# Loads of the DFT matrix issued by GpSimd behind the operation that frees their buffer, and a new order list, in a gated mix of a spectral layer and attention

## The chip, the core and the metric

The kernel runs on one core of a Trainium2 chip. Its time is device microseconds of one execution; 1714.48 us is the median of three before the change (1708.18 to 1717.01). The profile comes from one more execution of the same program, which took 1709.57 us, with a span of 1707.8 us from its first to its last instruction. Five engines run side by side, each through its own list of instructions in order: PE (TensorE, the matmuls, with its weight loads shown apart as PEld), DVE (VectorE), ACT (ScalarE), POOL (GpSimd) and SP (SyncE, which here issues DMAs). They wait for one another through semaphores.

## The reference

The output is a mix, by a gate for each row, of two results from the same x of 2048 rows and 640 columns. One is the real part of a two-dimensional DFT, written as matmuls. The other is attention with 32 heads of 20 that share one key and one value.

```python
g = sigmoid((x * gate_w).sum(-1, keepdims=True))
a = x @ dft_hid_re.T
b = x @ dft_hid_im.T
y = dft_seq_re @ a - dft_seq_im @ b
q = (x @ wq).reshape(B, S, 32, 20).transpose(0, 2, 1, 3)
k, v = x @ wk, x @ wv
p = softmax(einsum("bhqd,bkd->bhqk", q, k) * 20 ** -0.5)
o = einsum("bhqk,bkd->bhqd", p, v)
out = g * y + (1 - g) * (o.transpose(0, 2, 1, 3).reshape(B, S, 640) @ wo)
```

All is in float32. The kernel writes a float32 operand as the sum of two rounded parts, high and low, and leaves out the product of the low parts.

## The kernel before

**Stages.** First come the projections q, k, v and the gate, then the DFT over the hidden dimension (line 137), with the first score tiles between them. From 237 to 1537 us runs the main loop, which does three kinds of PE work together. A tail finishes the last head pair and the last DFT groups, and the projection by `wo` ends the program.

**Attention in the main loop.** Heads go in 16 pairs. For each pair the scores are computed twice. The "a" scores (line 363, tokens a to g and A to G of the list) only yield row maxima, by a reduction on DVE (line 370). When a pair's last maximum is there, `a_reduce` and `a_final` put the maxima in order on DVE (lines 389 to 407, result `ms`), `m_d<-ms` writes them to DRAM, and four small loads `qs<-m_d` bring them back as two more rows of the pair's q. The "b" scores (line 877, tokens h to n and H to N) use these rows, so the first b score of a pair waits for its `qs<-m_d`. ACT takes their exponential into `pt` (line 887), and the AV matmuls (line 901, token V) multiply it with v.

**The sequence DFT in the main loop.** The product with the DFT matrix is done in 7 products of half size (`PRODUCTS`), each in 8 groups; the main loop does the first 48 groups (`GMAIN`), the tail the rest. A group uses two halves (`sh` 0 and 1) of a row of blocks of the matrix. For each half, in products 0 to 4, two blocks of 512 KB are loaded into `craw0` and `craw1`, of which there is one buffer each. POOL adds the second to the first (line 522), which frees `craw1`, then makes the high part `ch` (line 532) and the low part `cl` (line 533), which frees `craw0`. Products 5 and 6 have one block a half, in the two buffers in turn. `ch` and `cl` have three buffers each. Below, "a split" is the addition, `ch` and `cl`. Once a group POOL also prepares a tile of x for the next product (lines 560 to 564, "the x part"), and it sums the parts that ACT takes out of PSUM (`ypart`, line 931) and the results in DRAM (`ya`, line 793), which go back by `y_d<-ya`. The DFT matmuls (line 737) take half of PE's rows: token 0 stands for rows 0 to 63, token 1 for rows 64 to 127, and a score on the other half of the rows runs beside them.

**What sets the order.** PE's order in the main loop is written out by hand in `PLAN`, a string of 10,456 characters with one token for each piece of work; "-" ends a part, behind which ACT empties the shared PSUM bank (`epoch`). ACT's, DVE's and POOL's operations stand in the order in which the recording of that list reaches them. DMAs are issued by `move` (line 118), from SP unless told otherwise, and SP issues them one after the other: an issue that waits for a buffer holds up all behind it. `load_c` issues a half's `craw` loads and is called by `f_stream` at the start of each half (line 823) and at its seventh step (line 826); `split_c` is called at its fifth step (line 828).

Of the kernel before, what the change touches and what calls it, by code (L numbers as in the profile page):

```python
# [34 lines left out]
def kernel(  # L35
# [488 lines left out]
    def split_c(g, sh):  # L524
        if g < len(GROUPS):
            eng = nc.vector if g > GMAIN else nc.gpsimd
            add_c(g, sh)
# [5 lines left out]
            eng.tensor_tensor(l, raw, h.bitcast(F32), op=ALU.subtract)  # L533
# [461 lines left out]
    def finish_last(ts, sm):  # L995
# [20 lines left out]
        "VVVVVNfe1i111c11k1h1111n1f11b1l1k1c111h1111fg1E1bVVVVVVV-GMajEdVVVVVVVhC11l1f111nk1bj111a1l111f11g11"
        "b1k111hCVVVV0H00B0N0D00C00M0H0I00G0L00D000000FJA00IgVVVVV-iFAJdeVVVVVVVDhJ0000F000EI0N00DA00C0F0I00l"
        "VVVVVLa11ci1k111m1g1111aI111lc11dnf11111a111blJVVVV-fLJkAnVVVVfJ111lka111g1i1FcVVVVViG0F0KH000jL0B0G"
        "000K00F00A00BcVVVVVVV-AfIklGVVVVIa00MK0E0000NC0H0B0000M0eD00cGVVVVVVVVJd11lm1g11i111a1dj11111e1g1mVV"
        "VV-FjEdiAVVVVVVV1dl1b111hf1111j11ke1g1111b1a1j1f11k111lVVVVV00L0A0I0D00M0000G0LH00C00B00DM0000L00NH0"  # L1020
        "0C00F0I000EVVVV-aJMIG000ED0A00J00000MNB00000ECVVVVVVVVVV1j1e1ig111a1m111j1l111i1d1n111f1h1c111eDVVVV"
        "VV-lHJNfiVVVVVVja11111Gm1l1d11i11jh11111fgVVVVVfJH0NB0000000KEJ00M0A00VVVVV-cDFlGiVVVVVV00I0FD0L0000"
        "N0J00H00FI00E0000DNVVVVVV1n11d1b11l11hm1g11111djl111i111a11111fg1jd11e11VVVV-nCFikHVVVVVVkMB1ja1gEVV"
        "VVVVjAN0M0B0000E000KAJ00000G0I0FVVVV-aJNbdLVVVVB0N00E00K0J0A000I0000G0FK000L0C000A0B0NVVVVVV1h11n11c"
        "i1e111m1a111d1n111c1il111f11hg11VVVVVV-FajLgIVVVVVV11l11gi1h11c11f11l1dg11i111c11h11e11mVVVVVV0C0M0L"
        "000G0A00K0JF000B0LG000000K0H000CFVVVV-GhkBjEVVVV0KG000J000B0L0A00D00GJ000MBeVVVVVVVVB1nf1d1lJ11hVV1e"
        "1m111c1ka11n111em111i1dc111n1111h1f111e1iVV-AcGkFbVVVVVVVVVVVmGC00H00I0K00E00NM00A000J00BVVVVV-iMgAC"
        "kVVVVVVKa00M0J0GB0000L00AK00M0000NJVVVVVVMa11n1d1j111l1ia111mg1111d1cVVVV-mGDBehVVVVVVVd11i111a1l111"
        "n1fk11i11c11la11g11f1111kjVVVVdN00L000FJ0A000I00GK0000L0M0CVVVVV-eDMbgHVVVVVVV00DIH000E00G00MJ00B000"
        "K00000E0MN0A00J0B000K0000EFVVVVVek11111i1fch111111ldn11111f1iac1111l1k1VVVV-HDejBmVVV11cl111m11kb1h1"  # L1030
        "111ge1111jfVVVVVVVVF00J0E000HN0D00000FJ000BH0E0000G0DJ00M0VVVVV-FenJIaVVVVGmJ0L0H000I00D0FnVVVVVVV1i"
        "n1111fa11k111ei1111jg1f1VVVVV-GjLiAdVVVVVhE1b11nd1j11f1111eh111n111icVVVVV0B00LN0J00MA000000B0ED00N0"
        "VVVVVV-eNIfkCVVVVVF00K000CI0G000L000MK00A0I00J00EN00000FAVVVVVf11h1g111j11ie111fh11d1111cn11ie11a111"
        "mVVVVVV-lFCidNVVVVVV1g1kc11i1m1111e11n1d111a1bj11f11l11g11kVVVVVVF00K000BNE00000HM0KC0000G0000BHE000"
        "00MCVVVV-fiAGLkVVVV0LF0H0000K0G00B000LF0A00J0KnVVVVVV1h11gk11mc1111ia111g11k1e1cMVVVVVV-EmgKa11jb111"
        "e1m111k1n11j111a1fVVVVVVVVmA000JG0EK00000BH0M0J00N00D0VVVVVKc00G0I0M00H00E0J000KB000G0FVVV-cIKaNeVVV"
        "VVVVVVVhG1d11j1l1b1111mga1111c1k1l1VVVVVV-AldNcmBVVVVVVc111m11di1na1111j11me111b1d11g11a1111jlVVVVVJ"
        "d00GL0I0000H0F00Ck00000LI0G00FH00000J0D00EG0000IF00HVVVVV-GaBLjdVVVVVVjA0ILG0000D00M0C000H00B000NEVV"
        "VVVVbN111cl1h11f11kn11b111lj11a1111f1d11ig11VVVV-bFkChLVVVVVVFh1lb111jd11n1111am111eb111jVVVVMa0JE00"
        "000IG0K0AmVVVVVV-FhKNbeVVVVVVG00LB00KH000000F00GL000C0DB0000AM0000LNVVVVV1lb1n111d1h11m11e1111b1nc1h"  # L1040
        "d1111m1l11g1b11VVVVV-enDFch11i11l11gVVVVVVVVVGjL0F00IH000K000C0G000E0M00BVVVVVVV-lMBdgHVVVVV0D0H00FN"
        "00I00E00K0AJ00000NM0000IE000K0AVVVVV1ai11f11k111l11g1a1i1c1111k11mg1l1b111a1k111c11fVVVVVV-AiDeCnVVV"
        "VV1n11k11a111eim1gj1111111dh11iVVVVVVI00AK00J0000G000M0IA0D000EN0000J0MH000BVVVVV-MceNAdVVVVVVL00G00"
        "HJ000F0D00000EI000ANcFVVVVVVVh1e1111j11g11i11mae11111j11k1b1g111mh1j111e1k111bf1VVV-jLhGBkVVVVVVVVVk"
        "A00IEN00J00F00H00K000IE000GVVVL00D0n0H0C0B00MVVVV-HcbMnDVVVVVVVdNI0F0J000H000EdGVVVVV1a1k11ec11111n1"
# [212 lines left out]
```

## Time and profile before

| what | us |
|---|---|
| median of three runs | 1714.48 |
| profiled execution | 1709.57 |
| its span | 1707.8 |
| PE, DVE, ACT, POOL busy in the span | 1687.7, 1449.2, 1227.8, 873.1 |
| main loop | 237 to 1537 |
| POOL busy in the main loop | 779.1 |

A row of a timeline gives start, duration, engine, line, operation, output and inputs, and how often; in brackets stands the idle time of the engine just ahead of it and what ended it as far as the profile can tell. A wait that names an engine which had long been done was another, often a DMA. A row of waits gives the total, the count and the longest. Windows give busy time by engine (with the number of instructions), then the granted clock of PE as a share of full speed, the share of time in which the DMA engines were busy, and GB/s. PE's matmuls are pipelined and their ends are modelled.

### The profile page before, as it was taken

How to read it: one execution, taken by the hardware profiler on the slowest of the kernel's cores; microseconds unless marked ns; L12 is line 12 of the kernel's file. 1: busy time of each engine (PE TensorE's matmuls, PEld its weight loads, DVE VectorE, ACT ScalarE, POOL GpSimd, SP SyncE). 2: the span in 40 equal slices, each digit the busy share in tenths (PEclk: the TensorE clock that was granted, in tenths of full speed). 3: DMA queues.
4: the chain of work that ended last, by engine and by line, in shares of the span. 5: the costliest groups of instructions: out<-in, count | busy, mean ns of one | idle time of the engine just before them, and what ended most of it. 6: DMA issues, size and time to landing. Idle time of an engine off the chain costs nothing.

```text
span 1707.8 us, 64072 instructions
## 1 busy us (share of the span) xinstructions
PE 1687.7 (99%) x27862; PEld 1480.6 (87%) x27862; DVE 1449.2 (85%) x2403; ACT 1227.8 (72%) x2499; POOL 873.1 (51%) x599
## 2 busy tenths in 40 slices
...
GB/s 295 239 179 113 149 111 106 109 132 96 133 122 154 125 149 111 152 117 175 110 152 145 161 98 126 134 150 128 161 123 144 94 135 77 106 104 165 207 204 259
DMA packets 139015, 245.38 MB, mean 144 GB/s; under 512 B 26716, under 2 KB 87996, under 8 KB 136212
## 3 DMA queue, kind: packets, MB, share of 16 engines
...
## 4 chain that ended last, share of the span: by engine, by line
PE 92%; DMA 3%; DVE 3%; issue 1%; POOL 0%; SPq 0%; ACT 0%; DVEq 0%; POOLq 0%
PE shared L901 27%; PE shared L737 17%; PE b L877 16%; PE a L363 16%; PE ab L137 7%; PE y_F L737 2%; PE q L126 1%; PE q L128 1%; PE q L127 1%; DVE mx L370 1%; PE av L959 1%; PE o L128 1%; PE o L126 1%; PE o L127 1%; DMA craw<-in_cre_dram 0%
## 5 line engine op out<-in xcount | busy, mean ns | idle before, releaser
L370 DVE TENSOR_REDUCE mx<-a 128x1 f32<-128x512 f32 x2048 | 1260.1, 681 | 112.7 <-PE a L363 85.0
L887 ACT ACTIVATE pt<-b 128x512 f32<-128x512 f32 x2048 | 1051.0, 615 | 215.5 <-PE b L877 153.6
L363 PE MATMUL a<-ks,qs 60*128 60x512 f32 x2048 | 673.3, 397 | 1.5 <-DVE mx L370 0.8
L877 PE MATMUL b<-qs,ks 62*128 62x512 f32 x2048 | 649.6, 397 | 8.3 <-DMA qs<-m_d 7.0
L737 PE MATMUL shared<-x,ch 64*128 64x320 f32 x3072 | 657.0, 301 | 0.3 <-ACT ypart L929 0.3
L737 PEld LDWEIGHTS shared<-x,ch 64*128 64x128 f32 x3072 | 497.7, 186 | 14.5 <-issue 9.1
L901 PE MATMUL shared<-pt,vsb 128*32 128x128 f32 x15360 | 492.7, 275 | 0.1
L901 PEld LDWEIGHTS shared<-pt,vsb 128*32 128x32 f32 x15360 | 399.2, 110 | 84.9 <-issue 49.4
L737 PE MATMUL shared<-x,cl 64*128 64x320 f32 x1536 | 459.6, 299 | 0.0
L877 PEld LDWEIGHTS b<-qs,ks 62*128 62x128 f32 x2048 | 343.7, 185 | 48.4 <-issue 22.4
L363 PEld LDWEIGHTS a<-ks,qs 60*128 60x128 f32 x2048 | 351.8, 185 | 32.3 <-DVE mx L370 11.1
L522 POOL TENSOR_TENSOR craw<-craw 128x1024 f32<-128x1024 f32 x80 | 189.7, 2371 | 242.0 <-DMA craw<-in_cre_dram 120.6
L737 PEld LDWEIGHTS shared<-x,cl 64*128 64x128 f32 x1536 | 285.8, 186 | 4.0 <-issue 2.8
L533 POOL TENSOR_TENSOR cl<-craw,ch 128x1024 fp32r<-128x1024 f32 x98 | 232.5, 2372 | 7.9
L931 POOL TENSOR_TENSOR ypart<-ypart 128x320 f32<-128x320 f32 x72 | 62.7, 871 | 225.8 <-ACT ypart L929 224.4
L532 POOL CAST ch<-craw 128x1024 fp32r<-128x1024 f32 x98 | 101.8, 1039 | 51.1 <-PE shared L737 27.4
L137 PE MATMUL ab<-wh,xh 64*128 64x320 f32 x640 | 124.3, 298 | 1.4 <-DVE both L608 0.9
L137 PE MATMUL ab<-wl,xh 64*128 64x320 f32 x640 | 123.5, 296 | 0.0
L137 PE MATMUL ab<-wh,xl 64*128 64x320 f32 x640 | 123.2, 296 | 0.0
L607 ACT ACTIVATE half<-ab 128x320 f32<-128x320 f32 x64 | 28.0, 437 | 105.6 <-PE ab L137 103.8
L137 PEld LDWEIGHTS ab<-wl,xh 64*128 64x128 f32 x640 | 89.2, 186 | 0.0
L137 PEld LDWEIGHTS ab<-wh,xl 64*128 64x128 f32 x640 | 89.2, 185 | 0.0
...
## 6 DMA issues: line engine op xcount, KB each, us to landing
...
xr<-x_d SPq DMA_DIRECT2D x88, 320.0 KB
...
```

Of the source, the lines that this page charges most:

```text
L126: nc.tensor.matmul(ps, wh, woven(xh), start=(i == 0), stop=False)
L137: nc.tensor.matmul(ps, w[r], woven(x[r]), start=(i == 0 and k == 0), stop=(i == n - 1 and k == 2))
L363: nc.tensor.matmul(ps, qs[p][b : b + 60, qb * P : (qb + 1) * P], woven(ks[b : b + 60, c * ROW : (c + 1) * ROW]), start=True, stop=True,)
L370: return nc.vector.tensor_reduce(mx[p][:, hh, qb, c : c + 1], ps, axis=AX.X, op=ALU.max)
L522: eng.tensor_tensor(raws[0], raws[0], raws.pop(1), op=PRODUCTS[GROUPS[g][0]][0][1])
L532: eng.tensor_copy(h, raw)
L533: eng.tensor_tensor(l, raw, h.bitcast(F32), op=ALU.subtract)
L737: mm = nc.tensor.matmul(ps[g % len(ps)], w, woven(x), start=start, stop=stop)
L877: nc.tensor.matmul(ps, ks[b : b + 62, kc * P : (kc + 1) * P], woven(qs[p][b : b + 62, qc * ROW : (qc + 1) * ROW]), start=True, stop=True,)
L887: halves.scored(nc.scalar.activation(t, ps, AF.Exp, scale=SCALE), n)
L901: mm = nc.tensor.matmul(acc[32 * g : 32 * g + 32], vsb[:, kc], t[:, g * VW : (g + 1) * VW], start=fresh, stop=end)
L931: nc.gpsimd.tensor_tensor(info["t"][0], info["t"][0], t, op=ALU.add)
```

## The change

`load_c` gets an argument for the issuing queue. For groups up to `GMAIN`, `split_c` now issues the next half's loads itself, from POOL: the load into `craw1` right behind the addition that frees it, the load into `craw0` right behind `cl`; where a half has one block, its load goes ahead of or behind the split, depending on the buffer. `f_stream` no longer issues them in the main loop, and still does in the tail. The very first split keeps its loads on SP. And `PLAN` is another string, of the same length and with the same number of each kind of token.

```diff
-    def load_c(g, sh, which=(0, 1), hold=None):
+    def load_c(g, sh, which=(0, 1), hold=None, queue=nc.sync):
...
-                ins = move(raw, (cre, cim)[i][th * SJ + k, sh])
+                ins = move(raw, (cre, cim)[i][th * SJ + k, sh], queue)
...
-    def split_c(g, sh):
+    def split_c(g, sh, ahead=True):
         if g < len(GROUPS):
             eng = nc.vector if g > GMAIN else nc.gpsimd
+            ahead = ahead and g <= GMAIN
+            one = len(c_raw[g, sh]) == 1
             add_c(g, sh)
+            if ahead and not (one and (g + sh) % 2):
+                load_c(g + sh, 1 - sh, which=(1,), queue=nc.gpsimd)
             raw = c_raw.pop((g, sh))[0]
...
             eng.tensor_tensor(l, raw, h.bitcast(F32), op=ALU.subtract)
+            if ahead:
+                load_c(g + sh, 1 - sh, queue=nc.gpsimd)
...
-            split_c(0, 0)
+            split_c(0, 0, ahead=False)
...
-                load_c(g + 1, sh)
+                if g >= GMAIN:
+                    load_c(g + 1, sh)
                 for j in range(SJ):
-                    if j == 6:
+                    if j == 6 and g + sh >= GMAIN:
                         load_c(g + 1 + sh, 1 - sh, which=(1,))
...
-        "hB11jdl111f11n11b111hc11dl1VVVVVCl1h1d11i11gm11lCVVVVmn1BEjkAVVVgI00jL0F000D00H0I0N000C00ME000HD000I"
...
```

Three places show what moves. The first is SP's list around the maxima of pair 8, in the main loop near 920 us of the profile (`craw` are loads of the DFT matrix, `xr` loads of x, `y_d<-ya` stores of results, `m_d<-ms` the store of the maxima). Before:

```order
L118 DMA craw<-in_cre_dram 128x1024 x2
L118 DMA xr<-x_d_70 128x640
L118 DMA xr<-x_d_69 128x640
L118 DMA y_d<-ya 128x320
L118 DMA m_d<-ms 128x64
L118 DMA craw<-in_cre_dram 128x1024
L118 DMA ya<-y_d 128x320
L118 DMA qs_865<-m_d 1x64x32 x4
```

SP's list at the same place now:

```order
L118 DMA xr<-x_d_70 128x640
L118 DMA xr<-x_d_69 128x640
L118 DMA y_d<-ya 128x320
L118 DMA m_d<-ms 128x64
L118 DMA ya<-y_d 128x320
L118 DMA qs_865<-m_d 1x64x32 x4
```

The `craw` loads are gone from SP's list, two ahead of the maxima and one between their store and their loads; the store `y_d<-ya` still stands ahead of `m_d<-ms`.

The second place is POOL's list just ahead of the `ya` that this store takes. Before, two splits follow each other, then the x part and the sums:

```order
L522 TENSOR_TENSOR craw<-craw 128x1024
L532 CAST ch<-craw 128x1024
L533 TENSOR_TENSOR cl<-craw,ch 128x1024
L522 TENSOR_TENSOR craw<-craw 128x1024
L532 CAST ch<-craw 128x1024
L533 TENSOR_TENSOR cl<-craw,ch 128x1024
L560 TENSOR_TENSOR xr<-xr 128x640
L563 CAST x_4_18372<-xr 128x640
L564 TENSOR_TENSOR x_4_18372<-xr,x_4_18372 128x640
L931 TENSOR_TENSOR ypart<-ypart 128x320
L793 TENSOR_TENSOR ya<-ypart,ya 128x320
```

POOL's list at the same place now, from the first of the two splits to the x part:

```order
L522 TENSOR_TENSOR craw<-craw 128x1024
L118 DMA craw<-in_cre_dram 128x1024
L536 CAST ch<-craw 128x1024
L537 TENSOR_TENSOR cl<-craw,ch 128x1024
L118 DMA craw<-in_cre_dram 128x1024
L522 TENSOR_TENSOR craw<-craw 128x1024
L118 DMA craw<-in_cre_dram 128x1024
L536 CAST ch<-craw 128x1024
L537 TENSOR_TENSOR cl<-craw,ch 128x1024
L118 DMA craw<-in_cre_dram 128x1024
L566 TENSOR_TENSOR xr<-xr 128x640
```

Each split issues two loads, and each load stands right behind the operation that frees its buffer; the sums `ypart` and `ya` follow behind the x part as before.

The third place is PE's list up to the first b score of pair 8, `b_8_0_0_1` (the numbers are pair, key block, query block and head of the pair; `a_592_1` is an a score, `x4_3` a tile of x). Before:

```order
L737 MATMUL shared_3908<-x3_3_15521,cl_18112 128x320
L363 MATMUL a_591_1_18849<-ks_82,qs0_863 128x512
L737 MATMUL shared_3908<-x4_3_16033,ch_18367 128x320 x2
L737 MATMUL shared_3908<-x4_3_16033,cl_18368 128x320
L737 MATMUL shared_3908<-x4_3_16033,ch_18367 128x320
L877 MATMUL b_7_14_3_1_18858<-qs1_864,ks_82 128x512
L877 MATMUL b_7_15_3_1_18862<-qs1_864,ks_82 128x512
L737 MATMUL shared_3908<-x4_3_16033,ch_18367 128x320
L877 MATMUL b_8_0_0_1_18867<-qs2_865,ks_82 128x512
```

PE's list up to the same score now:

```order
L743 MATMUL shared_3912<-x3_3_15542,cl_18118 128x320
L363 MATMUL a_588_1_18850<-ks_82,qs0_863 128x512
L743 MATMUL shared_3912<-x4_3_16033,ch_18369 128x320
L884 MATMUL b_7_15_3_1_18854<-qs1_864,ks_82 128x512
L743 MATMUL shared_3912<-x4_3_16033,ch_18369 128x320
L743 MATMUL shared_3912<-x4_3_16033,cl_18370 128x320
L884 MATMUL b_8_0_0_1_18860<-qs2_865,ks_82 128x512
```

In the fourth tile of x the score now comes behind three DFT matmuls instead of five, and behind three fewer a scores of this head (588 instead of 591 is the last ahead of it).

More of the change, by code (lines that the diff above doesn't have):

```diff
@@ L1016 @@
[L1016 to L1045, printed above, removed]
@@ L1111 @@
[L1111 to L1115 removed]
+        "Ai111jdl1m111g111ai1c1111k1l1n11fVVVc11kf1lBGh1VVVVVBh1EmknCVVVVV0D00C0Nl0fI00A00D0N00000C0LF000I00G"
@@ new lines @@
+        "00000H0D0L00I00J000MA00N000E0I0000D0C0H0fVVV-kBhGcLVVVVVVVeNj11a11bk111m1EnVVVbK1m11a1n1ej11111bd11f"
+        "1111hgVVVVVV-dHFbjLVVVVVmC11ek1bh1111g11j111md1111eaVVVVVVVd0L0MG0A00000C0I0D0E0NmVVVV-NcfBkHVVVVVVh"
+        "FK00B0000C0N0LF000000H0IDN0000JL0FaVVVFn1j1k1e11a11b1FgVVVVVVV-IadEmJVVVV1m1d11ja11e1i1111md111j11g1"
+        "1h111ie1f11jDVVVVVjE000FIG000K0A0J0E000B00F0K0VVVVVVV-eKbHCg00M000000K0E00IA000FJ00000KN000B0E0JVVVV"
+        "VVVVVMabj111g11l1k111f11a111ji1e11111n11d11fc11iAVVVVVVV-FkIeCgVVVVVVVlB11j1fd111n1a111l11i1111cn1f1"
@@ new lines @@
+        "1111lkaBVVVVVdMA00L0I000C0G00K000F0L0A00000BJ0D0000NLVVVV-GhbCeMVVVVVViF0JG000H000ED0I00M0C0G000A0Li"
+        "VVVVVIe111ncd11h1m1l1111111gj111h1b11fk111e1gVVVVV-KfLhbJGVVVVVaIe11j1g11111fkAiVVVVViG0M0D000LA0C00"
+        "nB000M000K00EAgVVVVVV-eiKFhCVVVVVKe00FH00IJg00D000E00000HM00BGcVVVVVVVbM11nea111j11d1f1i1111g1l1j1VV"
+        "VV-lDfCiAVVVVVVV1cmb1111h111d11lc1m111g1ia11111e1d111mjVVVVVJ00E0H000FK0G000J00L000A000ID000MJG00000"
+        "L0H0B00D00FVVVV-HbKECM0N0000HB0000D000LF00C00GVVVVVVVVVVgJm11dl1h11111b111n1jf11k1e111i1h1111f1gVVVV"
@@ new lines @@
+        "VV-AgImkLVVVVVV1m11d1n111ei1a1m111k11n11ceBVVVVJG0000E00KI000A000JN00FVVVVVV-nChIeKVVVVVVVV0B00K0LAJ"
+        "000G00B0K00M00A0000LCVVVVVlA1m1c11i11k1g11a1e1111m1j1b11111n1k1a1f1111j1l1gVVV-ChemDIVVVVVVVB11lkfJa"
+        "GVVVM0000D0LJ0A0000B0MG00D000LVVVVVV-NebMdHVVVV0F0I000A0K00N0E0F0I0000C0K000ANL00000BFVVVVVV1blh1111"
+        "fg1111j1111ie1d1fh11111cg1VVVVVV-FkaLjIVVVVVf11j111ail111d11111f1j1ni1111a1k1e1j1111m1gVVVVV0G0MC00K"
+        "0L0000B0G00M0H0D00000CE0I000M0GVVVVVV-EmCbKhVVVM00C00K0H0B0E0000F00C0K00NhBVVVVVGmc1hk1111b11l1gFVVV"
@@ new lines @@
+        "VVVn1e1i1111f11k1jg111111lb111hk1f111g11cVV-FhdBgLVVVVVVVVkE00BM0N00H0000JLD00M0000BG0VVVVVVVV-mNEbj"
+        "KVVVVViGJE000000K0M0A0NB00000J0L0DVVVVJb11d1n1lm111a1111bc111g1ke1VVVVVVV-CkGiFhVVVVg1i1111am11dj111"
+        "g11i1111efh11c111k11b1nVVVVVNfC0K0L00000IA0N00F00D00J0L0VVVVVVV-FeJgbHVVVVVVV0GH000EB0000J0M0000N00A"
+        "0E00CK000M000B00AN000K0E00MVVVVV1f1h111ek111bn11m1111aj1k11e111gi1m11a1VVVV-bnDLAfVVVVV11ld1h11n111b"
+        "111mj11l11d1aVVVVVVAL000C00K00FN0000HE00B0000KJ0G000M0H0E0VVVVV-MglhCBVVNF000eK000JH00BVVVVVViAl1c11"
@@ new lines @@
+        "111dm1n1a111i11e1c1m1VVVVVVVV-CeMBhnVVVm11he11111j1i1g1m11d1111ehVVVVVVVVVaL0M0KB0000GJ0000HE00F0I00"
+        "0DVVVV-HembCNVVVV0F0I000GJL0000A0M000B00D0J00NE0A00F000IVVVVVVVa11i11f1l11n11d11hi111c11l11fg1k111a1"
+        "1cVVVVV-KgAlfBVVVVVV1h1f111l1n1b1111ka1m111e11c1n1i11d111hfVVVV0A0KB000M0J00G00H0K000E000M0B0CN00A00"
+        "0EVVVVVV-AGjFbkVVVVVK00G0MC000H0I000K0000LM0G0CaVVVVVJe11m1n1a1d1i11l1j111m1a111gVVVVVV-fNjAlbd1111n"
+        "11111fja1111lb111nVVVVVVVV0I00AN00000EM00CI00H0G000KmEVVVVVKg0LF000HJ0000B0G0D0E000M0H0VVV-fNHcKbVVV"
@@ new lines @@
+        "VVVVVVVCkhf1111b11n111lc1d1h1111m1gVVVVVV-kFgHcEVVVVVV1n1c11hf11l11d11n1c111a1i1l111f11111knbJVVVVVV"
+        "bNC0M0K000000A0E0N00I0M0C000000KG0A0i00EM00J000D00N0BVVVV-gKclMAbVVVVVFj000HE0KB00000NC000FA000E0KVV"
+        "VVVVVf11h1dj111l11g111m11h1b1c11d1l1n11f11b1VVVV-gkLJmAVVVVVVlGh111cm11kb11111ge11a1j111mVVVVcNL00F0"
+        "00A00KB0jGVVVVVV-IjaKfEVVVVVV0D00M0EJ0000A00I0D0M000NCE0000I0A0F000KVVVVVVa11k11e1m1i1c111111hdn11f1"
+        "11lb1111j11hd1n11111feVVVV1g1-mDhcBlVVVVVVVViE0C0H000K0FN0000E0I000A0J0KVVVVVVVV-KaJBenVVVVV0B0N0E00"
@@ new lines @@
+        "J000K0A00IN00F0000J0L0D00A0I00FVVVVVVVVm11b11l111aj1k111f11i1e11g111ja11k1f111iVVV-DnBAclVVVVVi1111l"
+        "h11g1k1c111b11f11l1111gh11c1d1iLVVVVVVVCL0000DI0000G0M00J000EA000BK0M0000NJ00VVVV-gFHdcLVVVVVVVfLD00"
+        "0N0H00C0B00F000EN00D00HVVVVVV1m1a111lb11k1g1111m1alj1111b111kmg111l1111a111jb11dVVV-AlCmBnVVVVVVVVVI"
+        "g0C00M000HEK00nBVVVLa0D0J0N00I0000MA0L0C000D0G0VVVV-LckfIHVVVVV00MB0dC0H0000LGVVVV1l11c11dh1n111b1e1"
+        "1j1111maVVVVVVV-AFljB1nk111h1111ef1j11111n111i1k1e11af111jVVVVVVVVVJfK00HB00000LN00F0C000D0B00HVVVVV"
@@ new lines @@
+        "VV-dHBcgLVVVVVV0I00CL000DN00H00B0J00E000MD0N000A0I000C000L000MK00GVVVVVGm11j1d11l11ia11gm11111cd1e11"
+        "111h1b1n1m1VVVVV-EgmDhCVVVVVVHgk1fl1111c11b11a1n1k111f11lVVVVVhE0D00IM00000NJ0E0A00B00K00FVVVVV-ikcH"
+        "NEVVVVVVVlA00N0DJ00BF0000H00L0G0000KCVVVVVV1gk1111c1l11f1h11n1d1b11lc111hVVV-eDhIGmVVVViD11h1lgf1111"
+        "j1di111111agVVVVVVVVHbGK0000J00FL00000BH0D0G00J0VVVV-JaKBemVVVVV0I00F0000LDJ0H00B000FG0000EK000C0I00"
+        "0HVVVV11e1h11b1j111nd1m11h1111ecVVVVVVV-dAEiMgVVVVVV1hf1111l11bn111k1a111m1e11c1n1i1k11111a1f1e11g1c"
@@ new lines @@
+        "11iVVVVVLB000M0N00D00C00L000A0IF00N00000KL0C0B0VVVVV-cEkmNAVVVVVVVaN0FLK0000000CB00HN000EF000KVVVVVk"
+        "11e1m111g11i11h1ke11f11c1IgVVVV-IFkejHVVVVVVVV1he1j1111f1k1i1h111e11c11ndFVVVVVGj0K00H0EF000B00J0G00"
+        "0KVVV-JmdIhEVVVVVVV0B0H0LF00000K0J00IA0N00L00F000DVVVVnFd1i1l111c111am11g11i11d1l1VVVVV-gLbdh11fc11n"
+        "11l111111hb1d111111nm1e1111hcVVVVVVVVVCl0AM0000K0N00B0JE000F0000AK0000BGVVVVVVV-AfbKcLVVVVVLF000I000"
+        "0KAJ00EN0000B0M0000K00A0JL00000NB00FVVVVVVg1m1e11i11c1k11111n1f11a1i11e1k11jg11m1VVVVV-jLgmDAVVVVVVm"
@@ new lines @@
+        "d111h11e111n111jm1k11ai11gEVVVVVViGE0000K0MAC000gIVVVV-bHFljKVVVVEI000C000MK0000AL0B000G0M0000CD00A0"
+        "00LIVVVVVVKbl1111ch1g1111mid11111ej11hVVVVVV-JgkhB1lf1111cg1111k1b11a1111meVVVVVVVVVVhB000EM00NDJ000"
+        "0B0H000M000EGVVVVVV-EfgHIcVVVVV0I0F00N00H00EJ0B0K00G0000F000LA0JB0000KVVVVAj11d1m11bl11n11111cafKVVV"
+        "VVVV-AdCnmBVVVVVV11mc11dn111b11h1m1111j1eg1111kh11b11m1111l1c1dg111h1111ifVVVVVVGI00000FKA00L0000N0B"
+        "00J00D0F00LA00000NIVVVV-nFLdaIVVVVVV0B00H00D0LN0000M0I0A000C0LVVVVVjBe1m111a1n111k111bjf111e1n1VVVVV"
@@ new lines @@
+        "-MNcbEkVVVVV1n11d11ie1j11m111nd11i1h11eJVVVVVVHb0E0G0J00KF000000IAVVVVV-FINdejVVVVV00G0K00LC00B000M0"
+        "H000D0GC000LF000IVVVVVVV1j1fb111n111e1kc111m11a1n1VVVV-jGflKBVVVVe11m11d1i111cn11e11m1111hbd1111nj11"
+        "11meVVVVVV00E0MCK000000N0BH000F00E00J000K0G0B0H000F0CVVVVVV-BafNkLVVVVVA00K0L000FN00000IA000KC000LM0"
+        "00G0AVVVVVVa1m1111e1n1dj11111h1mb11n1e11jd11111hi1VVVVV-cNhEfdIVVVVVVi1f11h1k1111e1g1b111m1ac11LkVVV"
+        "VV0L0A000KbF0C0N0L0000A0KVVVVV-JDefaNVVVVV0L0G0000K0M0J000B0L00H0G00D00MVVVVVhDm11e11gj11111ik11a11f"
```

123 lines of the change are left out of this document (49 added, 74 removed).

## The prediction

> **What bounds the kernel now.** I read the page's first two lines, then PE's waits in the main loop, then the clock around its one long wait, then the chain through that wait.
>
> ```profile
> span 1707.8 us, 64072 instructions
> PE 1687.7 (99%) x27862; PEld 1480.6 (87%) x27862; DVE 1449.2 (85%) x2403; ACT 1227.8 (72%) x2499; POOL 873.1 (51%) x599
> PE b L877 <- DMA qs<-m_d: 7.0, 1, 7.0
> PE b L877 <- DVE mx L370: 1.1, 3, 0.5
> PE a L363 <- DVE mx L370: 0.8, 3, 0.3
> ```
>
> PE is busy for 99% of the span, so what a change of queues can win lies in the rest. The last three lines (time, count, longest) are PE's waits between 237 and 1537 us, the stretch that runs by the list PLAN. One is large: 7.0 us, once, for the small loads `qs<-m_d` that bring pair 8's row maxima. All the others come to about 2 us.
>
> ```profile
> 237.00:919.00 682.00, 680.81 (x12509) 592.72 (x12511) 628.33 (x1061) 550.87 (x1139) 413.36 (x269) 1.00 0.44 131
> 929.35:935.20 5.85, 5.85 (x71) 4.92 (x73) 0.69 (x1) 1.36 (x3) 0.00 (x0) 0.50 0.23 43
> 936.00:1537.00 601.00, 599.31 (x11111) 521.38 (x11108) 537.27 (x905) 487.03 (x1005) 357.12 (x249) 1.00 0.43 125
> 237.00:1537.00 1300.00, 1290.15 (x23750) 1122.78 (x23749) 1171.46 (x1975) 1044.01 (x2154) 779.10 (x523) 1.00 0.43 128
> ```
>
> These stretches list busy time of PE, PEld, DVE, ACT and POOL, then the granted clock, the DMA share and GB/s. The clock is 1.00 on both sides and 0.50 for the 5.85 us behind the wait. So the wait costs twice: while PE stands, and again while it runs at half speed.
>
> ```profile
> 921.98 2.36 POOL craw L522
> 924.36 0.33 SPq L118
> 925.22 0.61 SPq L118
> 927.13 2.08 DMA qs<-m_d
> 929.35 0.64 PE b L877
> ```
>
> The chain of waits (start, length, what) goes from an addition on POOL to an issue on SP, further issues, a landing and PE. SP issues in program order, and the issue at 924.36 is a load of the DFT matrix that waited for its buffer. Here is SP's own list, with the rows farther up in which such a load came late:
>
> ```profile
> 841.29 0.48 SPq L118 DMA_DIRECT2D craw<-in_cre_dram  x1
> 854.94 0.42 SPq L118 DMA_DIRECT2D craw<-in_cre_dram  x1
> 874.21 0.43 SPq L118 DMA_DIRECT2D craw<-in_cre_dram  x1
> ...
> 922.05 0.32 SPq L118 DMA_DIRECT2D y_d<-ya  x1
> 922.47 0.38 SPq L118 DMA_DIRECT2D m_d<-ms  x1
> 924.36 0.33 SPq L118 DMA_DIRECT2D craw<-in_cre_dram  x1
> ```
>
> And POOL's list (last bracket: idle time ahead, and who ended it by the profile):
>
> ```profile
> 821.66 0.87 POOL L931 TENSOR_TENSOR ypart<-ypart 128x320 f32<-128x320 f32 x1 [7.02 <-ACT ypart L929]
> ...
> 845.18 2.37 POOL L522 TENSOR_TENSOR craw<-craw 128x1024 f32<-128x1024 f32 x1 [10.23 <-PE b L877]
> ...
> 859.76 2.37 POOL L522 TENSOR_TENSOR craw<-craw 128x1024 f32<-128x1024 f32 x1 [8.65 <-DMA craw<-in_cre_dram]
> ...
> 865.64 1.55 POOL L560 TENSOR_TENSOR xr<-xr 128x640 f32<-128x640 f32 x1
> ...
> 869.56 0.88 POOL L931 TENSOR_TENSOR ypart<-ypart 128x320 f32<-128x320 f32 x1
> 870.52 1.70 POOL L793 TENSOR_TENSOR ya<-ypart,ya 128x320 f32<-128x320 f32 x2
> 878.06 2.38 POOL L522 TENSOR_TENSOR craw<-craw 128x1024 f32<-128x1024 f32 x1 [5.84 <-DMA craw<-in_cre_dram]
> ...
> 910.42 2.36 POOL L522 TENSOR_TENSOR craw<-craw 128x1024 f32<-128x1024 f32 x1 [4.23 <-DMA craw<-in_cre_dram]
> ...
> 921.16 0.86 POOL L793 TENSOR_TENSOR ya<-ypart,ya 128x320 f32<-128x320 f32 x1
> ```
>
> Each of SP's first three rows is followed by the addition that needs it: 841.29 to 845.18 is 3.89 us, 874.21 to 878.06 is 3.85. (The 10.23 us put down to PE are such a load too: line 522 waits for two loads and for nothing of PE.) So POOL lost 10.23, 8.65 and 5.84 us to late loads, fell behind, and reached `ya` at 921.16. SP holds the store `y_d<-ya` ahead of `m_d<-ms`; the maxima had been ready since 909.25:
>
> ```profile
> 909.03 0.22 DVE L407 TENSOR_REDUCE ms<-mt 128x32 fp32r<-128x64 f32 x1
> ```
>
> **The change part by part.** *Loads off SP.* Of 192 `craw` loads 175 move to POOL. SP loses 175 issues and, what counts, their waits in the main loop:
>
> ```profile
> SPq L118 <- POOL craw L522: 260.8, 62, 15.7
> SPq L118 <- POOL cl L533: 213.1, 66, 18.1
> ```
>
> Those 474 us were waits in which everything behind stood. They are no gain in themselves, since PE met only one of them.
>
> *Loads onto POOL.* What an issue costs there is seen in the ten `wraw` loads (group row: count, busy, mean ns; issue rows: KB, us to landing):
>
> ```profile
> L118 POOL DMA_DIRECT2D wraw<-in_wiT_dram x5 | 2.7, 538 | 16.2 <-DVE wl L168 13.7 <-DVE gz L261 2.5
> wraw<-in_wrT_dram POOLq DMA_DIRECT2D x5, 320.0 KB, 8.2
> wraw<-in_wiT_dram POOLq DMA_DIRECT2D x5, 320.0 KB, 4.4
> ```
>
> 175 issues at 0.54 us put 94 us on POOL. It is busy for 779 of 1300 us in the loop, so 867 if all fell there: room is left, and the price to PE is nothing as long as the 521 idle us cover it where they fall. The landing of a 512 KB load issued by POOL isn't in the trace. Below stand SP's 3.85 us for the same load, above it the 8.2 us of the slower `wraw` row. I take 5.5, an estimate: 4.4 for 320 KB, and about 1.1 for 192 KB more, somewhat under SP's 3.85 x 192 / 512 = 1.4, which has a fixed part in it. That keeps to the faster row, since four of the slower row's five were issued within 2.31 us at the start, as no loads of the loop are:
>
> ```profile
> 4.04 2.31 POOL L118 DMA_DIRECT2D wraw<-in_wrT_dram  x4
> ```
>
> *Is POOL in time for pair 8?* I walk its new order from 821.66, where it waited for ACT and so was on time. From the rows: a split with its addition takes 5.9 us (859.76 to 865.64), 7.0 with two issues; the x part 3.9 (865.64 to 869.56); `ypart` and two `ya` 2.7, with one `ya` 1.8. The next addition can start 5.0 us behind a split's end (5.5 less the issue itself). ACT's parts are ready by these rows, and PE's pace is taken as it was:
>
> ```profile
> 854.68 0.43 ACT L929 ACTIVATE ypart<-shared 128x320 f32<-128x320 f32 x1
> ...
> 873.95 0.43 ACT L929 ACTIVATE ypart<-shared 128x320 f32<-128x320 f32 x1
> ...
> 884.11 0.43 ACT L929 ACTIVATE ypart<-shared 128x320 f32<-128x320 f32 x1
> ...
> 907.73 0.54 ACT L929 ACTIVATE ypart<-shared 128x320 f32<-128x320 f32 x1
> ```
>
> Split 822.5 to 829.5, x to 833.4, `ypart` and `ya` to 836.1. Split to 843.1. Split 848.1 to 855.1 (before: from 859.76), x to 859.0, `ypart` and `ya` to 861.7. Split to 868.7 (before: from 878.06); now POOL waits for ACT, until 874.4. `ypart` to 875.3, split to 882.3, x to 886.2, `ypart` and `ya` to 888.9, split to 895.9. Split 900.9 to 907.9 (before: from 910.42), x to 911.8, `ypart` and `ya` to 913.6. Before, `ya` ended at 922.02: the chain to PE starts 8.4 us earlier, and it also loses the load at 924.36, which I count at nothing. PE asked for the maxima at 929.35 - 6.96 = 922.39. The new list has two DFT matmuls and an a score fewer ahead of that score, about 0.5 us of PE's work, so 921.9 is wanted and 929.35 - 8.4 = 920.95 is had. The wait goes, with 0.9 us to spare; landings of over 6.4 us would bring it back.
>
> *The new list.* PE's work is the same: both lists hold 8416 score and DFT tokens and 1920 AV tokens, in 347 AV runs; summing the longer of PE's two row halves in each stretch between runs gives 1,740,992 columns before and 1,740,864 now, 0.01%. Waits fall elsewhere, though. Without that DMA wait PE's waits were about 2 us, so I bound the reshuffle by none (-2) and three times as much (+4), and take 0. DVE, ACT and the tail behind 1537 us keep their operations: 0.
>
> **The sum.** The profiled execution took 1709.6 us, 1.8 more than its span. Minus 7.0 for the wait, minus half of 5.85, or 2.9, for the half clock: **1699.7**. That run lies 4.9 us under the median of three (1714.48), and I add nothing: those runs had the same queue, and a wait a few us longer in them goes too. If the 4.9 have another cause, it is 1704.6.
>
> **The rivals.** *The wait stays.* `y_d<-ya` still stands ahead of `m_d<-ms` on SP. If POOL isn't earlier, because its loads land in 8 us, the same walk ends at 922, and only the issue between `m_d` and `qs<-m_d` goes: 924.36 to 925.22 at most, so 1708.7. For it: the spare is 0.9 us. Against: the rows of 3.85 and 4.4. The Trainium skill (DMA: Bandwidth & Descriptors, section "Issuing engines are not separate DMA queues") speaks for it: all issuers share the same 16 DMA engines, and issuing from several saves only the short time of the issue. By that rule this is the outcome; the 474 us above speak against it, being in-order waits and not issue time. The Trainium skill (DMA: Bandwidth & Descriptors, section "Anatomy of one DMA — SWDGE (gpsimd) path") also fits 2.0 us plus bytes over 436 GB/s for loads from GpSimd, 3.2 us here by estimate, which would raise the spare to 3.2; no run here shows it yet.
>
> *POOL becomes the bound: slower.* In products 0 to 4 POOL has two splits, an x part and the additions for each group, and PE gives it 1300 / 48 = 27.1 us. The splits' 14.0, and twice the wait for a landing (less the 0.5 of the issue), exceed that from a landing of 7.1 us on. At 8.2 it is 29.4, 2.3 more in each of 40 groups, 92 us; three buffers of split data let POOL fall behind by some 20 us first: 1699.7 + 72 = 1772. Against it: the 8.2 us belong to the program's start alone.
>
> *The new list waits elsewhere.* The first score of a pair comes about as soon behind its maxima as before, so any pair can stand where 8 did, for a few us: 1704.
>
> **How the numbers follow.** Forecast 0.68; the wait stays 0.14 (1708.7); waits elsewhere 0.11 (1704); POOL as the bound 0.07. The range runs from 1695 (the -2, and a few waits too short to be listed) to 1709, which takes in two rivals and leaves out the slow one. About 0.5% is what a measurement of this kernel can tell from no change. Against the median, faster means under 1705.9; so faster has the forecast and half of the third case, 0.73, no change the rest of both rivals, 0.19, slower 0.08.
>
> **What would show it.** Right: no DMA wait of PE in the loop, clock 1.00 throughout, `m_d<-ms` issued within some 5 us of `ms` for pair 8, POOL's waits for `craw` far below 150 us, its splits some 10 us earlier around 860. Wrong: landings of `craw` beyond 6.4 us, a PE wait for POOL's `cl`, or a `qs<-m_d` wait at another pair.

## The result, and the profile after

The changed kernel takes **1699.28 us** (median of 6 runs, 1697.85 to 1702.81) against 1712.77 for the kernel before in the same comparison: a ratio of 0.9927, 95% interval 0.9906 to 0.9947. The profiled execution took 1698.06 us, 11.5 less than the one of before. One execution of e5_hop1, one of e9_act and one of the kernel before took far longer than all others (5860, 9553 and 2110 us), and the times and ratios below leave them out.

The page's first lines after, then the first two of PE's waits in the main loop (total, count, longest), then two windows (busy time of PE, PEld, DVE, ACT and POOL, clock, DMA share, GB/s):

```profile
span 1696.3 us, 63920 instructions
PE 1684.0 (99%) x27862; PEld 1478.0 (87%) x27862; DVE 1446.0 (85%) x2403; ACT 1228.6 (72%) x2499; POOL 973.1 (57%) x774
```

```profile
PE a L363 <- DVE mx L370: 1.1, 4, 0.4
PE b L884 <- DVE mx L370: 0.9, 3, 0.4
```

```profile
919.00:936.00 17.00, 16.98 (x316) 14.52 (x316) 14.67 (x25) 14.52 (x30) 8.57 (x8) 1.00 0.41 114
237.00:1537.00 1300.00, 1296.36 (x23863) 1128.41 (x23855) 1174.55 (x1977) 1053.57 (x2173) 881.85 (x699) 1.00 0.44 128
```

The wait of 7.0 us for `qs<-m_d` is gone, PE is busy for 16.98 of the 17 us around the place where it was, and the clock is 1.00 there. In the main loop's 1300 us PE is busy for 6.2 us more. SP's list at pair 8, and three of POOL's additions ahead of it:

```profile
912.06 0.32 SPq L118 DMA_DIRECT2D y_d<-ya  x1
912.47 1.39 SPq L118 DMA_DIRECT2D m_d<-ms  x1
914.77 0.32 SPq L118 DMA_DIRECT2D ya<-y_d  x1
915.14 2.52 SPq L118 DMA_DIRECT2D qs<-m_d  x4
```

```profile
847.74 2.35 POOL L522 TENSOR_TENSOR craw<-craw 128x1024 f32<-128x1024 f32 x1 [5.30 <-DMA craw<-in_cre_dram]
...
873.38 2.35 POOL L522 TENSOR_TENSOR craw<-craw 128x1024 f32<-128x1024 f32 x1
...
898.67 2.37 POOL L522 TENSOR_TENSOR craw<-craw 128x1024 f32<-128x1024 f32 x1 [3.55 <-DMA craw<-in_cre_dram]
```

`m_d<-ms` is issued at 912.47 instead of 922.47, because `y_d<-ya` ahead of it no longer waits for a late POOL. The loads now read as follows in the page (count, KB, median us to landing), and among POOL's waits there are two new groups, the short ones of an issue for the operation just ahead of it:

```profile
craw<-in_cim_dram POOLq DMA_DIRECT2D x94, 512.0 KB, 4.0
craw<-in_cre_dram POOLq DMA_DIRECT2D x81, 512.0 KB, 4.0
```

```profile
POOL craw L118 <- POOL cl L537: 24.9, 84, 0.3
POOL craw L118 <- POOL craw L522: 22.9, 77, 0.3
```

### The profile page after: what moved, and what is told of

Same layout as the page of the kernel before. It is cut to its first block, busy times and chain, and to the rows that moved or that the text cites. A ratio compares the mean times of both kernels' runs of the same rounds, so it can differ in the third digit from the quotient of the medians.

```text
span 1696.3 us, 63920 instructions
## 1 busy us (share of the span) xinstructions
PE 1684.0 (99%) x27862; PEld 1478.0 (87%) x27862; DVE 1446.0 (85%) x2403; ACT 1228.6 (72%) x2499; POOL 973.1 (57%) x774
## 4 chain that ended last, share of the span: by engine, by line
PE 93%; DVE 2%; DMA 2%; issue 1%; POOL 1%; ACT 0%; SPq 0%; DVEq 0%; POOLq 0%
PE shared L908 27%; PE shared L743 17%; PE b L884 16%; PE a L363 16%; PE ab L137 6%; PE y_F L743 3%; PE av L966 2%; PE q L126 1%; PE q L128 1%; PE q L127 1%; DVE mx L370 1%; DMA oraw<-rx_d 1%; PE o L128 0%; PE o L126 0%; PE o L127 0%
```

## The experiments

Ratios are to the kernel before, run on the same chip in the same comparison. "After" is the changed kernel's 1699.28 us and 0.9927.

### Loads alone, list alone

```diff
 e1_loads: the changed kernel with the old PLAN
 e2_list: the kernel before with the new PLAN
```

> The changed kernel with the old list PLAN: the loads alone. Theory (the in-order waits of SP for POOL are what cost): the wait of PE for qs<-m_d at pair 8 is gone, since POOL's sums end some 8 us sooner whatever the list; about 1700 us (1696 to 1704), clock 1.00 through the main loop. Rival (the new list brings the gain): the wait of some 7 us stays at pair 8, 1709 to 1713 us.

> The kernel before with the new list PLAN and all loads on SP. Theory: SP still stands behind POOL ahead of the maxima, so one wait of 5 to 9 us for qs<-m_d stays, with some 6 us of half clock behind it; 1708 to 1713 us. Rival (the list brings the gain): no such wait, about 1700 us.

Measured: the loads alone 1697.58 us, ratio 0.9920 (0.9900 to 0.9939); the list alone 1708.88, ratio 0.9988 (0.9973 to 1.0002). Rows of PE's waits in the main loop, first of the loads alone, then of the list alone:

```profile
PE b L884 <- DMA qs<-m_d: 1.0, 1, 1.0
```

```profile
PE b L877 <- DMA qs<-m_d: 5.8, 1, 5.8
PE shared L737 <- POOL cl L533: 1.9, 1, 1.9
...
PE shared L737 <- POOL ch L532: 0.9, 1, 0.9
```

The whole gain belongs to the loads, and the list is worth nothing that these runs can tell. With the loads alone the wait of 7.0 us isn't wholly gone: 1.0 us of it is left, at a clock of 1.00. The profiled execution of the list alone was its longest (1716.84 us) and shows what else can go wrong while the loads stand on SP: around 894 us PE waited 2.8 us for POOL's split data, with half clock behind it. The kernel before may meet the same in some executions, whose times spread from 1705 to 1717 us, but no profile of it shows that.

### One order of SP less: the store alone

```diff
 e3_ystore, against before
-                move(y_block(yb, k), ya)
+                move(y_block(yb, k), ya, nc.gpsimd)
```

> The kernel before, with the stores y_d<-ya alone issued by POOL behind ya, and the DFT loads left on SP. Theory (any in-order wait between the maxima and their loads costs): m_d<-ms is now issued some 8 us sooner, but the load at 924.36, which waits for an addition of POOL, still stands ahead of qs<-m_d, so the wait of PE at pair 8 stays at 5 to 8 us; 1707 to 1713 us. Rival (the store ahead of m_d<-ms is the whole cause): the wait goes, 1700 to 1702 us.

Measured: 1705.74 us, 0.9963 (0.9947 to 0.9979), a wait of 5.0 us at pair 8 and one of 1.3 at an earlier pair. SP's list at pair 8:

```profile
911.32 3.88 SPq L118 DMA_DIRECT2D craw<-in_cre_dram  x2
916.38 2.73 SPq L118 DMA_DIRECT2D xr<-x_d  x2
919.16 0.42 SPq L118 DMA_DIRECT2D m_d<-ms  x1
923.83 0.33 SPq L118 DMA_DIRECT2D craw<-in_cre_dram  x1
924.26 2.52 SPq L118 DMA_DIRECT2D qs<-m_d  x4
```

The mechanism is the theory's in part: with the store gone, the load between `m_d<-ms` and `qs<-m_d` still holds the maxima. But `m_d<-ms` went out 3.3 us sooner, not 8, since the loads ahead of it wait for POOL too. The time came out 1.3 us below the range: `qs<-m_d` starts 0.96 us sooner than in before (925.22) and PE asks 1.3 us later, so the wait is 2 us shorter, and the half clock behind it 2.9 us shorter.

### What the wait costs: putting it back

```diff
 e5_hop1 and e6_hop3, against the changed kernel: 1 and 3 tensors hop_d in DRAM
-        move(m_d[p], ms)
+        move(m_d[p] if p != 8 else hop_d[0], ms)
+        if p == 8:
+            for src, dst in zip(hop_d, hop_d[1:] + [m_d[p]]):
+                move(dst, src)
```

> The changed kernel, where the maxima of pair 8 alone take one more hop through DRAM: about 2.3 us later at PE (a landing of 2 and an issue), of which some 0.5 us is spare, so a wait of about 1.8 us at pair 8. Theory (the clock falls only behind a wait of several us, and then for a time that the wait's length doesn't set): clock 1.00 throughout, cost at most 1.8 us, 1699 to 1702 us. Rival (half clock for about as long as the wait, as before's 7.0 and 5.85 read): some 1.5 us of clock 0.50 behind it, 0.8 us more.

> The changed kernel, where the maxima of pair 8 alone take three more hops through DRAM: about 7 us later, a wait of 6 to 7 us at pair 8, as long as the one of before, with POOL and SP otherwise as changed. Theory (this one wait with its half clock is what the change removed from the profiled run): half clock of 3 to 7 us behind it, 6.5 plus 1.5 to 3.5, so 1707 to 1710 us, less than 1712 since the loads stay off SP. Rival (the gain lies elsewhere and PE makes the wait up later): under 1703 us.

Measured: one hop 1703.87 us, 0.9964 (0.9942 to 0.9986); three hops 1712.65 us, 1.0012 (0.9995 to 1.0028); both lie above the ranges of their theories. PE's waits, first with one hop, then with three:

```profile
PE b L888 <- DMA qs<-m_d: 3.1, 1, 3.1
```

```profile
PE b L888 <- DMA qs<-m_d: 8.6, 1, 8.6
```

So this one wait, put back alone with all loads on POOL, takes the gain away, though at 8.6 us it is 1.6 longer than the one of before. The profiled execution of three hops lies 14.4 us above the changed kernel's: 11.0 of them are this wait and its half clock, and up to 1.7 more are half clock near the program's start. Rows of its chain of waits (start, length, what):

```profile
914.92 3.97 DMA y_d<-ya
...
919.28 2.87 DMA hop_d<-hop_d
922.17 2.08 DMA hop_d<-hop_d
924.27 2.10 DMA m_d<-hop_d
```

The three hops take 7.1 us together (919.28 to 926.38), the 7 foreseen. The wait is longer still, mostly because the load `ya<-y_d` ahead of them on SP waits for the landing of the store `y_d<-ya`, which took 4.0 us here and 2.7 in the changed kernel. One hop took 3.1 us, and PE's wait is as long, which speaks for no spare at pair 8 in the changed kernel. Its landing records show it: the last `qs<-m_d` landed at 920.03, and the score began at 920.16, right behind the matmul ahead of it. The 1.0 us of the loads alone say the same.

My theory of a clock of 1.00 behind a short wait wasn't tested here, since the wait came out at 3.1 us and half clock followed. Windows from PE's first work behind the wait on, of one hop (a wait of 3.1 us), the store alone (5.0), three hops (8.6), and of two runs told below, e8_yxpool (14.2) and e12_yin (5.0):

```profile
924.12:927.40 3.28, 3.28 (x37) 2.54 (x41) 1.29 (x2) 1.19 (x2) 0.00 (x0) 0.51 0.49 166
```

```profile
928.66:931.60 2.94, 2.94 (x41) 2.46 (x45) 0.69 (x1) 0.60 (x1) 0.00 (x0) 0.50 0.14 35
```

```profile
931.69:936.50 4.81, 4.81 (x51) 3.60 (x53) 1.29 (x2) 1.19 (x2) 0.00 (x0) 0.50 0.24 50
```

```profile
941.80:947.20 5.40, 5.40 (x56) 4.14 (x58) 1.56 (x3) 1.50 (x3) 1.22 (x3) 0.50 0.80 255
```

```profile
1019.62:1026.60 6.98, 6.97 (x60) 5.85 (x62) 2.15 (x4) 3.13 (x6) 4.09 (x5) 0.52 0.74 234
```

Behind the wait, half clock lasts 2.9 to 6.7 us (the last window's 0.52 has 0.3 us of full clock in it) and doesn't grow with the wait, against the rival: two waits of 5.0 us are followed by 2.9 and 6.7. So each of these waits costs itself and another 1.5 to 3.4 us. By the clock records of the traces half clock begins in these runs ahead of PE's first work behind the wait, or less than 0.1 us behind it, and its whole stretches are 3.41, 6.83, 10.24 or 17.07 us long, which is 1, 2, 3 or 5 times 3.41. The Trainium skill (TensorE: Matmul & The Clock Gate, section "Part 1: The HAM clock gate") has the clock set by activity windows of about 3.4 us that run freely. These lengths agree with it.

Shorter waits, found in runs told below, went both ways. In e11_act_yx one of 1.6 us, ended at 572.25, was followed by a stretch of half clock that began 1.2 us later:

```profile
573.42:576.83 3.41, 3.41 (x46) 2.79 (x48) 1.42 (x3) 2.31 (x5) 2.85 (x4) 0.50 0.33 75
```

One of 1.9 us in e12_yin and one of 3.0 us in e10_act_after left the clock at 1.00. So my theory that a short wait leaves the clock alone doesn't hold in general.

### The queue without the place

```diff
 e4_place, against before (with the new PLAN)
-                load_c(g + 1, sh)
+                load_c(g + 1, sh, queue=nc.gpsimd if g < GMAIN else nc.sync)
...
-                        load_c(g + 1 + sh, 1 - sh, which=(1,))
+                        load_c(g + 1 + sh, 1 - sh, which=(1,), queue=nc.gpsimd if g + sh < GMAIN else nc.sync)
```

`load_c` has the argument `queue` of the change.

> The new list, the loads issued by POOL, but recorded at their old places: the second half's loads and those of the next group then stand behind the x part and the sums in POOL's list instead of ahead of them. Theory (POOL's time for a group decides): a group then costs POOL two splits of 5.9, x 3.9, sums 2.6, four issues with their short waits 1.7 and two landings of 4.3 that nothing covers, 28 to 29 us against the 27.1 that PE gives it; POOL falls behind, PE waits for cl, 1740 us (1702 to 1780). Rival (only the queue counts, not the place): 1700 us as the changed kernel, with no wait of PE for POOL.

Measured: 1788.45 us, 1.0449 (1.0426 to 1.0472), above the range. One group of POOL, from addition to addition, with the late issue in it, and PE's three main waits:

```profile
699.43 2.36 POOL L522 TENSOR_TENSOR craw<-craw 128x1024 f32<-128x1024 f32 x1 [5.47 <-DMA craw<-in_cre_dram]
...
713.25 2.37 POOL L522 TENSOR_TENSOR craw<-craw 128x1024 f32<-128x1024 f32 x1 [6.85 <-PE a L363]
...
726.21 0.57 POOL L118 DMA_DIRECT2D craw<-in_cre_dram  x1
731.41 2.36 POOL L522 TENSOR_TENSOR craw<-craw 128x1024 f32<-128x1024 f32 x1 [4.63 <-DMA craw<-in_cre_dram]
```

```profile
PE b L877 <- DMA qs<-m_d: 38.0, 6, 14.1
PE shared L737 <- POOL cl L533: 14.4, 10, 1.9
PE shared L737 <- POOL ch L532: 11.0, 7, 5.2
```

The theory holds, its size doesn't: this group took POOL 32.0 us, not 28 to 29, since the loads landed later: 6.85 and 4.63 us of idle time ahead of its second addition and the next group's first, where I had 4.3 each. (The 6.85 put down to PE are a load too: it was issued at 705.85, right behind another, and landed at 713.11.) Medians of landing are 4.6 and 5.0 us instead of 4.0. On POOL's queue the place decides: the same queue with the loads behind the x part and the sums is 89 us slower. The new place on SP's queue wasn't run. And even where POOL is late, most of what PE waits for is `qs<-m_d`, by way of SP: 38.0 us, against 25.4 for POOL's `cl` and `ch`.

### SP freed further, POOL loaded further

```diff
 e7_ypool, against the changed kernel
-                move(y_block(yb, k), ya)
+                move(y_block(yb, k), ya, nc.gpsimd)
 e8_yxpool: that, and in load_x
-                move(raw, x_d[ie][:, 2 * jj : 2 * jj + 2].rearrange("p a b -> p (a b)"))
+                move(raw, x_d[ie][:, 2 * jj : 2 * jj + 2].rearrange("p a b -> p (a b)"), nc.gpsimd)
 e12_yin: that, and in y_in
-                move(t, y_block(old, k))
+                ins = move(t, y_block(old, k))
+                if (n, k) == (3, 1):
+                    tc.add_manual_dep(ins.ins, put[8].ins.name, ORDER, reason="behind the maxima")
```

Here `put[8]` is the last `qs<-m_d` of pair 8, so the load of `ya` for group 25 goes out behind it.

> The changed kernel with the stores y_d<-ya issued by POOL too, behind ya, so that only the loads of x keep SP waiting for POOL. POOL gets up to 1.7 us more for a group, 27.0 us in the fullest groups against the 27.1 that PE gives. Theory (nothing on SP reaches PE any more, and POOL's limit isn't passed): 1696 to 1702 us, as the changed kernel; m_d<-ms of pair 8 is issued sooner than 5 us behind ms. Rival (POOL is already at its limit): waits of PE for cl, 1703 to 1720 us.

> As the run before, with the loads of x issued by POOL as well: SP waits for POOL nowhere in the main loop, m_d<-ms goes out right behind ms for every pair. POOL gets 1.1 us more, 28.1 us in the 8 groups with two sums, some 26.4 in the others with additions. Theory (a backlog of 8 us in 8 groups fits into the 20 us of split data that POOL is ahead): 1695 to 1702 us. Rival (POOL's limit is passed): waits of PE for cl and half clock, 1705 to 1740 us.

> The run e8_yxpool (1716.3 us; POOL late, m_d<-ms issued right behind ms, but one load ya<-y_d, which waits for POOL, ahead of qs<-m_d of pair 8 on SP) with this one load of group 25 made to stand behind the four qs<-m_d; its data are wanted a group later. POOL's work is the same. Theory (the in-order wait on SP is the link by which POOL's lateness reaches PE): the wait of 14.2 us and the half clock behind it go, waits for POOL's cl of 3 to 5 us stay, 1698 to 1705 us. Rival (POOL is past its limit, and the time comes back as waits for cl): 1710 to 1716 us.

Measured: 1710.43 us, 0.9994 (0.9980 to 1.0008); 1716.30 us, 1.0038 (1.0023 to 1.0054); 1711.86 us, 1.0001 (0.9988 to 1.0015). All three miss their theory's time, and land in the range of their rival. In e7_ypool PE's one long wait in the main loop is for `qs<-m_d`, 11.2 us at pair 8. POOL's rows, then SP's:

```profile
871.43 2.37 POOL L522 TENSOR_TENSOR craw<-craw 128x1024 f32<-128x1024 f32 x1
...
898.41 2.39 POOL L522 TENSOR_TENSOR craw<-craw 128x1024 f32<-128x1024 f32 x1
...
922.98 0.57 POOL L118 DMA_DIRECT2D y_d<-ya  x1 [0.30 <-POOL ya L799]
```

```profile
921.37 0.38 SPq L118 DMA_DIRECT2D m_d<-ms  x1
925.11 0.32 SPq L118 DMA_DIRECT2D ya<-y_d  x1
```

The group takes 26.98 us, the 27.0 foreseen, and POOL isn't past its limit: PE waits for no `cl`. But in the changed kernel the same stretch, from 873.38 to 898.67, takes 25.3, and the eight groups of product 2 with two sums each lie just ahead of pair 8. So POOL reaches the store 11 us later than the changed kernel's `ya`, and SP, freed of the store, stands at the loads of x instead, so that `m_d<-ms` goes out 14 us behind `ms`, and then at `ya<-y_d`, which waits for that store to land. In e8_yxpool only this last load is left ahead of `qs<-m_d`, and it alone stands in their way for 21 us:

```profile
914.81 0.32 SPq L118 DMA_DIRECT2D m_d<-ms  x1
935.96 0.32 SPq L118 DMA_DIRECT2D ya<-y_d  x1
```

In e12_yin that one load is put behind the maxima. SP's list at pair 8, then at pair 9:

```profile
911.96 0.33 SPq L118 DMA_DIRECT2D m_d<-ms  x1
913.42 2.51 SPq L118 DMA_DIRECT2D qs<-m_d  x4
```

```profile
998.45 0.33 SPq L118 DMA_DIRECT2D m_d<-ms  x1
1013.76 0.32 SPq L118 DMA_DIRECT2D ya<-y_d  x1
1014.18 2.52 SPq L118 DMA_DIRECT2D qs<-m_d  x4
```

The wait of 14.2 us at pair 8 is gone altogether, with POOL's work unchanged, and PE's waits for `cl` are 4.3 us as the theory said: the time didn't come back as waits for POOL, as its rival had it. The same link then shows at pair 9, where the next `ya<-y_d` stands between: a wait of 5.0 us. The profiled execution (1716.48, 4.6 above the median) also has 4.0 us of waiting for DVE's split in the tail, with half clock behind it, that e8_yxpool's hasn't. So the link on SP is shown at pair 8, and the 1698 to 1705 us aren't: they would need every such load out of the way, which no run tried.

### The maxima on ACT

```diff
 e9_act on before, e10_act_after on the changed kernel, e11_act_yx on e8_yxpool
-        move(m_d[p], ms)
-
+        if p:
+            later(2, put_m, p, ms)
...
+    def put_m(p, ms):
+        move(m_d[p], ms, nc.scalar)
+        later(3, put_q, p, nc.scalar)
...
```

`put_q` issues the four `qs<-m_d` by ACT; `later` counts pairs of a scores. Pair 0 stays on SP.

> The kernel before, with all loads and stores of the DFT left on SP, and only the maxima taken off it: m_d<-ms and the four qs<-m_d of each pair are issued by ACT, a few exponentials behind the maxima, so that nothing that waits for POOL stands ahead of them. Theory (the in-order wait on SP is the link by which POOL's lateness reaches PE): no wait for qs<-m_d at pair 8 although POOL's splits are as late as before; 1698 to 1704 us, with at most 3 us of waits for POOL's cl. Rival 1 (POOL must be earlier, whatever the queue): waits of PE for cl of 5 us and more, 1708 to 1713. Rival 2 (the issues on ACT cost): 16 times some 3 us of ACT delay the exponentials, waits of PE for pt, over 1705.

> The changed kernel with the maxima of each pair issued by ACT, as in the run before. The changed kernel's profile has no wait left for qs<-m_d, so theory: the same time within the measurement, 1696 to 1700 us, and closer together, without the executions at 1702 to 1703 (clock 0.998 to 0.999), if these are a short wait at pair 8. Rival (the issues on ACT cost): 1702 to 1708.

> Loads of the DFT matrix, loads of x and stores y_d<-ya on POOL (the run e8_yxpool, 1716.3 us, POOL late), and the maxima on ACT. Theory (e8_yxpool lost its time in the in-order wait for ya<-y_d ahead of qs<-m_d, not in POOL's own lateness): the wait of 14.2 us at pair 8 goes, waits for cl of 2 to 4 us with some half clock stay, 1699 to 1706 us. Rival (POOL is past its limit): waits for cl grow to 10 us and more, 1712 to 1720.

Measured: 1761.31, 1768.59 and 1755.93 us, ratios 1.0299 (1.0270 to 1.0329), 1.0349 (1.0321 to 1.0377) and 1.0271 (1.0247 to 1.0295). All three miss their theory's time by far: the rival came, that the issues on ACT cost. No wait for `qs<-m_d` or for POOL's `cl` is left in the main loop of any, but PE waits for exponentials instead, so these runs say nothing on the link. What costs is not the issue time. ACT at pair 7 of e10_act_after, and SP:

```profile
837.46 10.04 ACTq L118 DMA_DIRECT2D qs<-m_d  x4
847.55 0.60 ACT L907 ACTIVATE pt<-b 128x512 f32<-128x512 f32 x1 [9.55 <-DMA xr<-x_d]
```

```profile
842.18 0.32 SPq L118 DMA_DIRECT2D xr<-x_d  x1
```

Four issues of 0.6 us take 10 us. By the trace's instruction list the DMAs issued by SP and by ACT take turns on the same eight semaphores, and an issue first waits until the DMA that had its semaphore before has landed; the fourth one here, at 846.96, waits for the load of x that SP issued at 842.18 behind its own waits. ACT was tied to SP's order again, and the exponentials with it.

## Why the prediction was right

**The wait goes, and half clock with it: right.** Both terms are seen: 6.96 us of wait and 2.9 of half clock are 9.9 of the 11.5 us between the two profiled executions. Another 1.1 is a wait for DVE's `cl` in the tail that the profile of before has and the one after hasn't; 0.5 stays unexplained. The half clock was a term of the right size for before's execution, but its length can't be forecast from the wait: the rows above have 1.5 to 3.4.

**The sum: right by 1.6 us in the profiled execution (1699.7 against 1698.06) and by 0.4 in the median (1699.28).** The near hit in the median is in part luck. I had left the 4.9 us by which the median of before lay above its profile out of the sum, as going too. By the six runs it lay 3.2 above, and the changed kernel's lies 1.2 above, so 2.0 went; what they consisted of isn't shown.

**POOL's walk: right in its outcome, by errors that offset one another.** Expected additions at 848.1, 861.7, 875.3 and 900.9; measured 847.74, 861.90, 873.38 and 898.67. The issues on POOL were undersized. The 173 in the loop took 97.5 us, 0.56 each, and 47.8 us more went in short waits of 0.3 us for the operation just ahead, which I hadn't counted, so that a split with its issues took 7.6 us (847.74 to 855.35), not 7.0. (My 867 for POOL's busy time was also added up wrong: 779 and 94 are 873. Measured: 881.85.) The landing was oversized: 4.0 us in the median instead of 5.5, and the two that nothing covered here held POOL for 5.30 and 3.55 us instead of 5.0 each. The Trainium skill's fit (DMA: Bandwidth & Descriptors, section "Anatomy of one DMA — SWDGE (gpsimd) path"), 3.2 us by estimate, lies 0.8 us under this median. From the sum `ypart` at 872.54 on, these errors cancel to 0.3 us. `ya` still came 1.6 us sooner than walked, because this `ypart` began 1.9 us sooner: ACT's part for it was ready at 872.45, not 874.4. In the loop POOL's idle time ahead of its additions fell from 230.0 to 103.6 us.

**The spare of 0.9 us: wrong, it is nought.** What failed is "PE's pace is taken as it was". The maxima came to PE 0.8 us sooner than I walked (920.16 instead of 920.95): `ya` was 1.6 sooner, and the chain behind it took 8.1 us instead of 7.3. But PE asked for them 1.7 us sooner, at 920.16 instead of 921.9. With the old list and the new loads it asked at 921.61, so some 1.4 us go with the new list, where I had 0.5 (and had counted one a score fewer ahead of that score, where the lists show three). The other 0.8 us by which it asked sooner than in before came with the old list too, and their cause stays open. That the wait went wholly, and not all but the 1.0 us of e1_loads, is luck.

**The new list at 0: right**, by the two runs that part it from the loads.

**The rivals.** *POOL as the bound*: the stretch from 873.38 to 898.67 took POOL 25.3 of the 27.1 us that PE gives it on average, so it had some 1.8 to spare. With 1.7 more (e7_ypool) PE still waited for none of POOL's data; with more again it did, for 2.9 us (e8_yxpool) and 4.3 (e12_yin). The threshold of 7.1 us for a landing holds only where the x part and the sums stand beside a landing and not ahead of its issue: in e4_place POOL was the bound with medians of 4.6 and 5.0. *The wait stays*: it was close, as the spare shows, and e7_ypool brings back more than the whole wait. The rule that issuing from several engines saves only the time of the issue (the Trainium skill, DMA: Bandwidth & Descriptors, section "Issuing engines are not separate DMA queues") is too narrow here: what was saved is what stood behind an issue's wait, and e12_yin saves a wait of 14.2 us by the place of one load on the same queue. *Waits elsewhere*: the profile after has none over 0.5 us in the main loop. But two of the six executions took 1702.38 and 1702.81 us, at a clock just below 1.00, and no profile shows where they lost it.
